# The first weight loads of a two-problem attention kernel: one chunk split over two queues, one moved ahead of a transposing load, two merged

## The chip, the cores and the metric

One core of a Trainium2 chip. The sessions ran on different chips (8, 4 and 1; that of the first result is not on record), and each ratio compares with the kernel before on the same chip. The metric is the device time of one execution in microseconds. In the traces, times count from the start of the span.

## The reference, cut to what matters

Two independent problems, A and B, each grouped-query attention with a key/value cache; only A's first projection, `x @ wq`, matters here. Its contraction over D = 1024 is done in eight chunks of 128.

```python
def _A_ref(x, k_cache, v_cache, wq, wo):      # x: (16, 32, 1024), wq: (1024, 32*128), bf16
    q = (x @ wq).reshape(B, Sq, Hq, Dh).transpose(0, 2, 1, 3)
    k = jnp.repeat(k_cache, rep, axis=1); v = jnp.repeat(v_cache, rep, axis=1)
    p = softmax(einsum("bhqd,bhkd->bhqk", q, k) * Dh ** -0.5)
    o = einsum("bhqk,bhkd->bhqd", p, v)
    return o.transpose(0, 2, 1, 3).reshape(B, Sq, Hq * Dh) @ wo
# ... B the same; the two results side by side
```

## The kernel before: the parts that matter

`w0` holds the weights of the first eight heads (NF = 6, then 6 and 7), `xT` the transposed x. Chunks 0 and 1 of x are transposed by TensorE, the others by transposing loads. ScalarE and SyncE issue loads.

```python
load_x(TT // 2, TT, nc.scalar)
nc.scalar.preload_act_table_set("natural_log_exp_and_others")
load_x(0, TT // 2)
load_w0(0, 1, 0, NF // 2)                 # chunk 0, heads 0-2, SyncE
load_w0(0, 1, NF // 2, NF, nc.scalar)     # chunk 0, heads 3-5, ScalarE
load_w0(1, 2, 0, NF)                      # chunk 1            "w1"
load_w0(2, 3, 0, NF, nc.scalar)           # chunk 2            "w2"
load_x_transposed(2)                      # x, chunks 2 and 3  "xT2"
load_w0(3, 4, 0, NF)                      # chunk 3            "w3"
load_w0(0, HC, NF, REP)                   # heads 6, 7 of chunks 0-3
load_w0(HC, HC + 1, 0, REP)               # chunk 4            "w4"
load_x_transposed(HC)                     # x, chunks 4 and 5  "xT4"
load_w0(HC + 1, DC - 1, 0, REP)           # chunks 5 and 6
load_x_transposed(HC + 2)                 # x, chunks 6 and 7  "xT6"
load_w0(DC - 1, DC, 0, REP)               # chunk 7
...                                       # [cut: later weights, K, V]
warm_up(22)                               # 22 matmuls on a constant
...                                       # [cut: transposes of chunks 0 and 1 of x]
first_heads(range(NF // 2, NF), (0,))     # [cut: heads 0-2 of chunk 0, in two halves]
first_heads(range(NF), (1, 2, 3))         # six matmuls per chunk
first_heads(range(NF, REP), range(HC))    # heads 6, 7: eight matmuls
first_heads(range(REP), range(HC, DC - 1))  # eight per chunk
...                                       # [cut: chunk 7, copies; then heads 8 to 31 among the attention work]
```

## Time and profile before

| | before |
|---|---|
| time, median of the first 3 runs | 343.4 us (343.21 to 343.67) |
| span of the profiled execution | 341.1 us |
| TensorE busy | 334.5 us, 98% |
| first matmul of chunk 1 / of head 8 | 6.28 / 18.80 us |

To read profile lines: PE is TensorE's matmuls, PEld its weight loads, ACT ScalarE, DVE VectorE, POOL GpSimd, SP SyncE; a q marks the engine's queue of instructions, and "issue" in a chain is time in which nothing that the profile shows was waited for. TensorE is the bound from end to end, so a change pays only where TensorE waits. The prediction below shows the only wait on data, 0.6 us for w1. SyncE's queue gives the order of issue (start, us, queue, line, operation; x2 merges two issues):

```profile
0.74 0.45 SPq L465 DMA_DIRECT2D x_sb<-in_A_x_dram  x1
1.26 0.92 SPq L474 DMA_DIRECT2D w_sb<-in_A_wq_dram  x2
2.22 1.44 SPq L468 DMA_TRANSPOSE xT<-in_A_x_dram  x1
3.71 1.60 SPq L474 DMA_DIRECT2D w_sb<-in_A_wq_dram  x3
5.35 1.47 SPq L468 DMA_TRANSPOSE xT<-in_A_x_dram  x1
```

All of these are issued long before their data is used; what decides is when they land.

### The profile page before, as it was taken

To read this page: it belongs to the slowest core of one execution; us is meant where nothing else is said; L and a number is where in the kernel's file an instruction comes from. 1 tells how busy PE (TensorE), PEld (TensorE's weight loads), DVE (VectorE), ACT (ScalarE), POOL (GpSimd) and SP (SyncE) were. 2 spreads that over 40 slices of the span, in tenths; PEclk is the share of its full clock that TensorE was granted. 3 is DMA by queue.
4 is the path that set the end of the run, shared out by engine and by line. 5 is a ranking of instruction groups with operands and counts; after the bars stand their busy time and mean duration, and the time that the engine had idled before them with its cause. 6 is when DMAs were issued, how large, how long until landed. Compare 5 with 4: busy or idle time off the path is not lost.

```text
span 341.1 us, 5436 instructions
## 1 busy us (share of the span) xinstructions
PE 334.5 (98%) x2074; PEld 212.8 (62%) x2113; DVE 265.4 (78%) x335; ACT 185.3 (54%) x208; POOL 47.0 (14%) x206
## 2 busy tenths in 40 slices
PE   8999999999999999999999999999999999999996
PEld 5455666666666666666666666666666666666555
DVE  0047988888988898888888988879888888889540
ACT  2057666666667667666645545555554555555110
POOL 0001110011111111110012221222122101111100
PEclk9999999999999999999999999999999999999999
DMA  7999999999996998899999955998449995430001
GB/s 199 298 188 274 288 250 225 205 254 250 301 258 144 241 222 232 197 294 308 322 293 290 240 125 147 338 284 222 118 106 307 357 194 152 115 93 9 17 19 33
DMA packets 128622, 71.70 MB, mean 210 GB/s; under 512 B 76880, under 2 KB 127824, under 8 KB 128592
## 3 DMA queue, kind: packets, MB, share of 16 engines
q1 hardware_dynamic: 127504, 69.78, 82.5%
q0 software_dynamic: 384, 1.05, 0.8%
q10 hardware_dynamic: 704, 0.49, 0.5%
q8 instruction: 17, 0.28, 0.3%
q14 instruction: 13, 0.11, 0.1%
HBM read 50.59 MB, written 2.10 MB: 154 GB/s over the span
## 4 chain that ended last, share of the span: by engine, by line
PE 96%; DMA 2%; issue 1%; ACT 0%; SPq 0%; ACTq 0%
PE f_ps L320 31%; PE q_ps L301 28%; PE ob L425 17%; PE s_ps L357 16%; PE q_ps L531 4%; DMA w_sb<-in_A_wq_dram 1%; DMA out_dram<-o_sb 0%; ACT o_sb L329 0%; SPq L465 0%; SPq L474 0%; ACTq L329 0%; ACT p_sb L365 0%; ACTq L365 0%
## 5 line engine op out<-in xcount | busy, mean ns | idle before, releaser
L365 ACT ACTIVATE p_sb<-s_ps,shift 128x1024 bf16<-128x1024 f32 x128 | 142.7, 1115 | 97.5 <-PE s_ps L357 86.3
L376 DVE TRANSPOSE_TENSOR_REDUCE parts<-p_sb 128x32 f32<-128x1024 bf16 x128 | 158.7, 1240 | 20.8 <-ACT p_sb L365 19.3
L320 PE MATMUL f_ps<-wo_sb,oT 128*128 128x512 bf16 (+1 forms) x524 | 127.6, 366 | 0.6
L301 PE MATMUL q_ps<-xT,wq_sb 128*128 128x512 bf16 x430 | 113.0, 379 | 0.6
L425 PE MATMUL ob<-p_sb,v_sb 128*128 128x256 bf16 x512 | 76.8, 273 | 0.8
L357 PE MATMUL s_ps<-qT,kT 128*128 128x256 bf16 x512 | 76.8, 273 | 0.0
L320 PEld LDWEIGHTS <-oT 128*128 128x128 bf16 x544 | 53.2, 98 | 35.3
L357 PEld LDWEIGHTS <-kT 128*128 128x128 bf16 x512 | 56.9, 113 | 28.3
L301 PEld LDWEIGHTS <-wq_sb 128*128 128x128 bf16 x448 | 43.8, 98 | 32.2
L425 PEld LDWEIGHTS <-v_sb 128*128 128x128 bf16 x512 | 50.1, 98 | 20.0
L447 DVE TENSOR_TENSOR oT<-r,ob 128x512 bf16<-128x512 f32 x64 | 43.9, 686 | 19.8 <-PE ob L425 19.4
L411 DVE STREAM_TRANSPOSE r<-rall 128x512 f32<-128x512 f32 x64 | 44.2, 691 | 1.1
L309 ACT CAST qT<-q_ps 128x512 bf16<-128x512 f32 x56 | 32.7, 583 | 16.5 <-PE q_ps L301 16.5
L394 POOL COPY half<-cs 64x32 f32<-64x32 f32 x32 | 6.6, 206 | 231.5 <-DVE cs L384 231.4
L329 ACT CAST o_sb<-f_ps 128x512 bf16<-128x512 f32 (+1 forms) x17 | 9.5, 559 | 23.6 <-PE f_ps L320 23.6
L531 PE MATMUL q_ps<-xT,w_sb 128*128 128x512 bf16 (+1 forms) x66 | 14.1, 369 | 0.6 <-DMA w_sb<-in_A_wq_dram 0.6
L406 DVE RECIPROCAL rall<-sums 128x32 f32<-128x32 f32 x32 | 10.4, 326 | 3.3 <-POOL sums L403 3.3
L384 DVE TENSOR_REDUCE cs<-parts 128x32 f32<-128x128 f32 x32 | 12.1, 377 | 1.1
L553 DVE CAST qT<-q_ps 128x512 bf16<-128x512 f32 x4 | 2.5, 683 | 13.2 <-PE q_ps L531 13.2
L531 PEld LDWEIGHTS <-w_sb 128*128 128x128 bf16 x67 | 6.4, 97 | 8.0 <-DMA w_sb<-in_A_wq_dram 1.1
L553 ACT CAST qT<-q_ps 128x512 bf16<-128x512 f32 x4 | 2.1, 599 | 12.8 <-PE q_ps L531 12.8
L331 POOL DMA_DIRECT2D out_dram<-o_sb x8 | 4.6, 575 | 29.2 <-ACT o_sb L329 29.2
(25 smaller groups left out, 48.1 us busy)
## 6 DMA issues: line engine op xcount, KB each, us to landing
v_sb<-in_A_v_cache_dram SPq DMA_DIRECT2D x16, 512.0 KB, 5.4
wq_sb<-in_B_wq_dram SPq DMA_DIRECT2D x8, 1024.0 KB, 6.0
wo_sb<-in_A_wo_dram SPq DMA_DIRECT2D x8, 1024.0 KB, 7.5
v_sb<-in_B_v_cache_dram SPq DMA_DIRECT2D x16, 512.0 KB, 4.6
wo_sb<-in_B_wo_dram SPq DMA_DIRECT2D x8, 1024.0 KB, 8.5
wq_sb<-in_A_wq_dram SPq DMA_DIRECT2D x5, 1024.0 KB, 6.7
wq_sb<-in_A_wq_dram SPq DMA_DIRECT2D x2, 512.0 KB, 7.3
kT<-in_A_k_cache_dram SPq DMA_TRANSPOSE x64, 4.4
```

The costliest lines, as they stand in the source:

```text
L301: nc.tensor.matmul(ps[:], lhsT=w[:, dc, (h % 4) * DH:(h % 4 + 1) * DH], rhs=xT[pr][:, dc, :], start=(dc == 0), stop=(dc == DC - 1),)
L309: nc.scalar.copy(out=qT[pr, g][:, :, hl, :], in_=ps[:].rearrange("p (b s) -> p b s", s=SQ),)
L320: nc.tensor.matmul(ps[:, 0:width], lhsT=oT[pr, tt][:, h, :], rhs=wo_tiles[pr, nh, h // REP][:, h % REP, off:off + width], start=(h == 0), ...
L357: nc.tensor.matmul(s_ps[:, c, :], lhsT=kT[:, i % GRP, c, :], rhs=qT[pr, g][:, b, :, :].rearrange("p h s -> p (h s)"), start=True, stop=True,)
L365: nc.scalar.activation(out=p_sb[:], in_=s_ps[:], func=ACTF.Exp, bias=shift[:], scale=SCALE)
L376: nc.vector.tensor_reduce(out=parts[k][:, q, :, :].rearrange("p c h -> p (c h)"), in_=st[i]["p"][:].rearrange("p c (h s) -> p (c h) s", s=SQ),
L384: nc.vector.tensor_reduce(out=cs[:], in_=parts.pop(k)[:].rearrange("p q c h -> p q h c"), axis=AX.X, op=ALU.add,)
L406: nc.vector.reciprocal(out=rall[:, k, :], in_=quad.pop(k)[:])
L411: nc.vector.transpose(out=r[:].rearrange("p n s -> p (n s)"), in_=rall[:, k, o * 2 * REP:(o + 1) * 2 * REP] .unsqueeze(2).to_broadcast([P, ...
L425: nc.tensor.matmul(ob[j][:, q, :], lhsT=v_sb[:, i % GRP, c, :], rhs=st[i]["p"][:, c, :], start=(c == 0), stop=(c == KC - 1),)
L447: nc.vector.tensor_tensor(out=out, in0=rcp.pop(j)[:].rearrange("p (q h) s -> p q h s", h=REP), in1=ob.pop(j)[:].rearrange("p q (h s) -> p ...
L531: nc.tensor.matmul(first_q[h][:, ts], lhsT=w0[dc // HC][:, dc % HC, h * DH:(h + 1) * DH], rhs=xT[0][:, dc, ts], start=(dc == 0 and t0 == 0 ...
```

## The change

The intent: w1 is what TensorE waits for, and it shares the DMA engines with w2, so bring w1 in with both queues at once and w2 behind it. Chunks 5, 6 and 7 become one load.

```diff
-            load_w0(1, 2, 0, NF)
-            load_w0(2, 3, 0, NF, nc.scalar)
+            load_w0(1, 2, 0, NF // 2)
+            load_w0(1, 2, NF // 2, NF, nc.scalar)
+            load_w0(2, 3, 0, NF)
             load_x_transposed(2)
... [cut: three unchanged loads]
             load_x_transposed(HC)
-            load_w0(HC + 1, DC - 1, 0, REP)
+            load_w0(HC + 1, DC, 0, REP)
             load_x_transposed(HC + 2)
-            load_w0(DC - 1, DC, 0, REP)
```

## The prediction

> **What bounds the kernel now.** I read the page first, then the list of waits, the chain of waits over the first 20 us, and the DMA view in narrow windows. The page:
>
> ```profile
> PE 334.5 (98%) x2074; PEld 212.8 (62%) x2113; DVE 265.4 (78%) x335; ACT 185.3 (54%) x208; POOL 47.0 (14%) x206
> ...
> PE 96%; DMA 2%; issue 1%; ACT 0%; SPq 0%; ACTq 0%
> ```
>
> TensorE is the bound: busy 98% of the 341.1 us span, and 96% of the chain that ended last. The change touches no matmul, only first loads, so it can win only TensorE's idle time. The list of waits of TensorE (waiter, releaser, us in total, times, longest) is two lines long:
>
> ```profile
> PE q_ps L513 <- PEq L687: 0.9, 1, 0.9
> PE q_ps L531 <- DMA w_sb<-in_A_wq_dram: 0.6, 1, 0.6
> ```
>
> The 0.9 us is the start before the warm-up. The 0.6 us is what the change aims at; in the chain (start, us, what) it is:
>
> ```profile
> 1.75 4.48 DMA w_sb<-in_A_wq_dram
> 6.23 0.05 issue
> 6.28 2.33 PE q_ps L531 x10
> 8.61 0.05 issue
> 8.66 10.31 PE q_ps L531 x47
> ```
>
> A load issued at 1.75 us, the second chunk's rows (192 KB on SyncE), lands at 6.23; from 6.28 on TensorE runs without a break. Later delays of loads are hidden now. I name chunks 0 to 7 of the projection's contraction: w1 is the second chunk's weights, w2 the third's, xT2 the transposing load of chunks 2 and 3 of x.
>
> Of the DMA view, windows holding one issue each give KB and us from issue to landing. The lines that carry the argument, in order of issue (the 256 KB one issued at 4.80 and the second transpose at 5.35 share a window):
>
> ```profile
> w_sb<-in_A_wq_dram ACTq DMA_DIRECT2D x1, 96.0 KB, 3.0
> ...
> w_sb<-in_A_wq_dram SPq DMA_DIRECT2D x1, 192.0 KB, 4.5
> w_sb<-in_A_wq_dram ACTq DMA_DIRECT2D x1, 192.0 KB, 4.7
> ...
> xT<-in_A_x_dram SPq DMA_TRANSPOSE x1, 5.2
> ...
> w_sb<-in_A_wq_dram SPq DMA_DIRECT2D x1, 256.0 KB, 5.0
> xT<-in_A_x_dram SPq DMA_TRANSPOSE x1, 5.5
> ...
> w_sb<-in_A_wq_dram SPq DMA_DIRECT2D x1, 512.0 KB, 5.5
> ```
>
> Added to the issue times of the timeline (1.34, 1.75, 1.83, 2.22, 4.80, 5.35, 6.87) they land at: w0's second half 4.34, w1 6.2, w2 6.5, xT2 7.4, w4 9.8, xT4 10.85, w5 with w6 12.4. So w1, issued first, lands only 0.3 us before w2: they moved side by side. What the engines moved per stretch (last two columns: DMA share, GB/s):
>
> ```profile
> 3.00:4.00 1.00, 1.00 (x11) 0.68 (x9) 0.17 (x1) 0.00 (x0) 0.00 (x0) 1.00 0.99 323
> ...
> 5.00:6.00 1.00, 0.68 (x4) 0.10 (x1) 0.00 (x0) 0.00 (x0) 0.00 (x0) 1.00 1.19 195
> ```
>
> The engines are full in both, but from 5 to 6 us, where w2 on ScalarE's queue runs against xT2 on SyncE's, they move 195 GB/s in place of 323.
>
> **What the Trainium skill says.** "DMA: Bandwidth & Descriptors", section "Issuing engines are not separate DMA queues": all issuers use the same 16 DMA engines and interleave, so a second issuer saves only issue time. Section "Queues, rings and completion order": each engine takes turns between rows, packet by packet. The trace agrees: w1 and w2, one per queue, land together. Splitting w1 thus makes no bandwidth; what helps is that w2 no longer takes half of it while w1 is awaited. The same page, "Latency and other measured facts", gives a transposing load 261 GB/s; here xT4 landed 1.05 us behind w4, 262 kB in 1.05 us or 250 GB/s, so it agrees. "Perfetto Trace Analysis", section "Tensor Engine Instruction (MATMUL, LD_WEIGHTS)": a matmul's end is an estimate. It shows: a 512-column matmul is written 379 ns long, but 58 of them started between 6.28 and 18.80, which is 0.216 us each. I count in 0.216.
>
> **The change, part by part.**
>
> (1) What there is to win. The last matmul of chunk 0 starts at 5.29 (end 5.67 less its modelled 0.38). The next could start at 5.29 + 0.216 = 5.51, and started at 6.28. Ceiling: **0.77 us**, a little more than the 0.6 listed.
>
> (2) w1 earlier. Its halves (96 KB each) follow the two halves of w0 in the two queues, with nothing beside them. 197 kB at the 323 GB/s of the row above is 0.6 us after 4.34: lands near 4.95. Chunk 1 starts at 5.51, not held by data: the 0.77 us go.
>
> (3) The next demand is chunk 2, six matmuls later: 5.51 + 6 x 0.216 = 6.81. It needs w2 and xT2. w2 now precedes xT2 in SyncE's queue: another 0.6, near 5.6. xT2 is issued one plain issue (about 0.46 us) later, at 2.7, but its bytes waited for the engines anyway. Undisturbed it takes the 1.05 us of xT4: 5.6 + 1.05 = 6.65. As a check, w1, w2 and xT2 took 7.42 - 4.34 = 3.08 us before; my sum is 2.25 to 2.3, the saving being the slow stretch. I add 0.1 to 0.4 for what I cannot resolve: xT2 at 6.75 to 7.05. Before, chunk 2 started at 6.28 + 1.30 = 7.57; now near 7.0, **a gain of 0.5 to 0.6**, part of the 0.77 being taken by xT2.
>
> (4) Chunk 5 now waits for a merged load, w5 to w7 (768 KB for 512 KB). Its extra 256 KB at the rate of the 512 KB (1.5 us between the landings of xT4 and w5/w6) cost 0.75 us: 12.4 + 0.75 less the 0.4 to 0.6 the stream is ahead, near 12.65. Need: 28 matmuls after chunk 2 starts (6 + 6 + 8 for heads 6 and 7 + 8 of chunk 4), 7.0 + 28 x 0.216 = 13.05. Free, by 0.4 only. Chunk 6's transpose, now behind w7, lands near 13.6, needed at 14.8: free.
>
> (5) SyncE: one issue fewer (about 0.58 us), ScalarE: the same count. Every load keeps its place in time from the next weights on. Bytes and matmuls are unchanged. The tightest later load I found, the 1 MB issued at 20.46, landed at 26.2 and is needed near 27.2, a margin of 1 us. So the gain of the start should reach the end undiminished, as TensorE waits for nothing afterwards.
>
> Sum: 343.4 - 0.5 = **342.9 us**.
>
> **The rivals.**
> (a) xT2 takes the place of w1 as the wait. For it: it is issued 0.46 later, and chunk 2 wants it 0.77 earlier. If it landed at 7.42 as before, 0.15 us would be won (343.25); if the later issue went through in full (7.88), 0.3 would be lost (343.7). Against: the queue, not the issue, held it, since 5.2 us passed from issue to landing and the later transposes do no better.
> (b) The merged w5 to w7 becomes the wait. For it: the thin 0.4 us of (4), and semaphores that need the slowest DMA engine. Against: the stream runs ahead. A late engine there could cost 0.2 to 1 us (343.1 to 343.9).
> (c) The load is hidden anyway, or the gain is lost at a later load. Against: TensorE did wait, and has no second wait to fall into. It would leave 343.4.
> (d) Everything works and xT2 is in time: 0.77 us, 342.6.
>
> **Range and chances.** (d) and the full loss of (a) are about 1.1 us apart and the three times of before spread over 0.46 us, so 342.5 to 343.5 should hold it 8 times in 10. Even the ceiling is 0.2% of the time, a tenth of the threshold: faster by 2% is impossible by this account, slower by 2% needs 7 us and only an unseen fault gives it.
>
> **What would show it.** In the changed profile: the DMA view should have both halves of w1 landing near 5.0; the chain should no longer hold a 4.5 us load of weights, but perhaps a short wait for xT; chunk 1 should start near 5.5 and chunk 2 near 7.0; the projections of head 8 should start near 18.25 rather than 18.80; no wait in the middle of the first projections at 12.5 to 13.5. A wait of TensorE for xT that ends after 7.4, or one for weights near 13, makes the prediction wrong; so does a span that does not follow the start of head 8.

## The result, and the profile after

| | before | after |
|---|---|---|
| median, 6 runs each | 343.31 us (342.94 to 343.67) | 343.27 us (342.7 to 343.92) |
| ratio after / before | | 0.9999, interval 0.9986 to 1.0012 |
| span of the profiled execution | 341.1 us | 341.5 us |
| first matmul of head 8 | 18.80 us | 19.20 us |

The range held (342.5 to 343.5), but the half microsecond forecast at its centre is not there. The page of the changed kernel, TensorE and the chain that ended last:

```profile
PE 335.3 (98%) x2074; PEld 213.3 (62%) x2113; DVE 265.4 (78%) x335; ACT 185.4 (54%) x208; POOL 47.1 (14%) x206
...
PE 95%; DMA 2%; issue 1%; SPq 1%; ACT 0%; ACTq 0%
```

The list of TensorE's waits has lost its second line:

```profile
PE q_ps L513 <- PEq L687: 0.9, 1, 0.9
```

One might call that success. The chain of waits says otherwise (start, us, what):

```profile
2.64 0.04 issue
2.69 5.25 DMA xT<-in_A_x_dram
7.93 0.04 issue
7.98 1.02 PE q_ps L531 x4
```

A DMA is in the chain again: xT2 in place of w1. It lands at 7.93, and chunk 2 starts at 7.98, where the kernel before started it at 7.58. The wait list does not show it because a matmul's modelled end (379 ns for one that takes 216 ns of the array) covers a short wait. The DMA view, windows of one or two issues (KB, us to landing):

```profile
w_sb<-in_A_wq_dram SPq DMA_DIRECT2D x1, 96.0 KB, 4.6
w_sb<-in_A_wq_dram ACTq DMA_DIRECT2D x1, 96.0 KB, 4.7
...
w_sb<-in_A_wq_dram SPq DMA_DIRECT2D x1, 192.0 KB, 4.7
xT<-in_A_x_dram SPq DMA_TRANSPOSE x1, 5.2
```

Half the bytes took as long as the whole before: the halves of w1, issued at 1.75 and 1.83, landed at 6.3 and 6.5, where w1 had landed at 6.2. And the slow stretch that the prediction laid to w2 running against xT2 is still there (TensorE alone, then its clock, DMA share, GB/s):

```profile
4.00:5.00 1.00, 1.00 (x8) 1.00 0.66 170
5.00:6.00 1.00, 1.00 (x5) 1.00 1.78 250
6.00:7.00 1.00, 1.00 (x6) 1.00 0.63 131
```

One more difference sits in TensorE itself. Weight loads of the stretch from 4.2 to 6.4 us (count, busy us, mean ns), the kernel before:

```profile
L531 PEld LDWEIGHTS <-w_sb 128*128 128x128 bf16 x10 | 0.9, 96 | 1.3 <-DMA w_sb<-in_A_wq_dram 1.1
```

and the changed kernel:

```profile
L531 PEld LDWEIGHTS <-w_sb 128*128 128x128 bf16 x10 | 1.3, 141 | 1.1 <-DMA w_sb<-in_A_wq_dram 0.4 <-issue 0.3
```

The same instruction takes 96 ns in one and mostly 151 in the other. TensorE ran chunk 0 slower in this execution, though no instruction of it was changed. One trace of each kernel was evidently not enough.

### The profile page after: what moved, and what is told of

It reads as the page before. It is cut to its first block, busy times and chain, and to the rows that moved or that the text cites. A ratio compares the mean times of both kernels' runs of the same rounds, so it can differ in the third digit from the quotient of the medians.

```text
span 341.5 us, 5437 instructions
## 1 busy us (share of the span) xinstructions
PE 335.3 (98%) x2074; PEld 213.3 (62%) x2113; DVE 265.4 (78%) x335; ACT 185.4 (54%) x208; POOL 47.1 (14%) x206
## 3 DMA queue, kind: packets, MB, share of 16 engines
q0 software_dynamic: 384, 1.05, 0.8%
## 4 chain that ended last, share of the span: by engine, by line
PE 95%; DMA 2%; issue 1%; SPq 1%; ACT 0%; ACTq 0%
PE f_ps L320 31%; PE q_ps L301 28%; PE ob L425 17%; PE s_ps L357 16%; PE q_ps L531 3%; DMA xT<-in_A_x_dram 2%; DMA out_dram<-o_sb 0%; SPq L474 0%; ACT o_sb L329 0%; SPq L465 0%; ACTq L329 0%; ACT p_sb L365 0%; ACTq L365 0%
## 5 line engine op out<-in xcount | busy, mean ns | idle before, releaser
L447 DVE TENSOR_TENSOR oT<-r,ob 128x512 bf16<-128x512 f32 x64 | 43.9, 686 | 19.8 <-PE ob L425 19.4
L531 PE MATMUL q_ps<-xT,w_sb 128*128 128x512 bf16 (+1 forms) x66 | 15.1, 388 | 0.2
```

Of the source, the lines that this page charges most:

```text
L447: nc.vector.tensor_tensor(out=out, in0=rcp.pop(j)[:].rearrange("p (q h) s -> p q h s", h=REP), in1=ob.pop(j)[:].rearrange("p q (h s) -> p ...
L531: nc.tensor.matmul(first_q[h][:, ts], lhsT=w0[dc // HC][:, dc % HC, h * DH:(h + 1) * DH], rhs=xT[0][:, dc, ts], start=(dc == 0 and t0 == 0 ...
```

## The experiments

Twelve more runs were made, all correct: each of the two kernels twice again, and eight variants. Two theories were to be told apart. **Theory one:** xT2 is the new wait because of its own cost: it slows whatever is beside it and is issued later. **Theory two:** the start is slow and uneven by itself; the order of the loads only decides which load the unevenness hits, and TensorE's own start varies too. All traces are summed up in one table; I read the starts from the records of the matmuls, and a load's landing from the last of its 16 completion counts. The second column is the start of the last weight load that took over 140 ns.

| trace | last slow load | w1 landed | xT2 | w3 | w4 | chunk 1 starts | chunk 2 | chunk 3 | chunk 5 | head 8 | span |
|---|---|---|---|---|---|---|---|---|---|---|---|
| before | 3.59 | 6.23 | 7.39 | 8.21 | 9.77 | 6.28 | 7.58 | 8.88 | 13.62 | 18.80 | 341.1 |
| before_again | 6.39 | 6.26 | 7.38 | 8.10 | 9.84 | 6.80 | 8.09 | 9.39 | 14.14 | 19.32 | 341.6 |
| before_third | 5.80 | 6.09 | 7.17 | 8.19 | 9.72 | 6.40 | 7.69 | 8.99 | 13.74 | 18.92 | 341.2 |
| merge_only | 6.45 | 6.19 | 7.34 | 7.85 | 9.70 | 6.74 | 8.04 | 9.33 | 14.08 | 19.26 | 341.6 |
| after | 5.81 | 6.34, 6.53 | 7.93 | 8.57 | 10.27 | 6.39 | 7.98 | 9.27 | 14.02 | 19.20 | 341.5 |
| after_again | 4.38 | 6.32, 6.49 | 7.84 | 8.55 | 10.25 | 6.37 | 7.88 | 9.18 | 15.13 | 20.32 | 342.6 |
| after_third | 4.31 | 4.88, 5.50 | 6.62 | 8.69 | 10.29 | 5.61 | 6.91 | 8.73 | 13.81 | 19.00 | 341.3 |
| after_no_merge | 5.16 | 4.83, 5.62 | 6.75 | 8.88 | 10.51 | 5.98 | 7.27 | 8.93 | 13.69 | 18.87 | 341.6 |
| w2_sync_only | 5.13 | 5.58 | 7.23 | 9.03 | 10.51 | 6.04 | 7.34 | 9.08 | 13.84 | 19.02 | 341.3 |
| split_only | 4.59 | 5.54, 5.80 | 6.66 | 8.85 | 10.31 | 5.73 | 8.66 | 9.97 | 14.72 | 19.90 | 342.6 |
| split_both | 5.16 | 5.01, 5.28 | 7.68 | 8.06 | 9.79 | 6.00 | 7.73 | 9.02 | 13.77 | 18.95 | 341.6 |
| early_transpose | 3.98 | 6.84, 5.41 | 6.57 | 8.40 | 10.10 | 6.89 | 8.19 | 9.49 | 15.71 | 20.90 | 343.2 |
| late_transpose | 6.36 | 5.82, 6.01 | 9.21 | 7.22 | 10.06 | 6.79 | 9.25 | 10.54 | 15.36 | 20.56 | 342.9 |
| all_sync | 3.45 | 5.48 | 7.36 | 8.54 | 10.04 | 6.14 | 7.44 | 8.73 | 13.48 | 18.66 | 341.1 |

**Everything is decided before head 8.** In ten of the fourteen traces the span less the start of head 8 is between 322.3 and 322.4 us; from head 8 to the last matmul all fourteen take 318.96 us. after_no_merge, split_only and split_both end 0.35 to 0.45 us later, after the last matmul (all_sync: 322.44). This goes with the number of transfers that a program issues: these three issue 177 or 178, all others 175 or 176. Why is open, but their ratios below contain it, so they overstate what their start lost. A trace of the start says what the load order did.

**A rival that is not tested: the chip.** before_again, after_again, late_transpose and early_transpose ran on chip 8, merge_only, after_no_merge, w2_sync_only and split_only on chip 4, split_both, all_sync, before_third and after_third on chip 1. With w1 split or w2 out of its way (early_transpose, where xT2 goes first, left aside), w1 landed at 5.8 to 6.5 us in after and on chip 8, and at 4.8 to 5.8 on chips 4 and 1. What sets after_third apart from the other two traces of the changed kernel may thus be the chip and not the run; as far as the record tells, no kernel was traced twice on one chip.

### The two kernels again: before_again, before_third, after_again, after_third

No edit. Expected of the kernel before:

> The kernel before, unchanged, for a second trace of the same start. If the start is the same each time: second chunk's weights (w1) land at 6.2 us, chunk 1 starts at 6.3, chunk 2 at 7.6, the first matmul of head 8 starts at 18.8. If the start varies from run to run by some tenths of a microsecond (the theory that explains why the changed kernel's times spread over 1.2 us): one of these moves by over 0.2 us, and the moment at which a weight load in TensorE's first microseconds drops from 151 to about 96 ns (3.9 us in the first trace of this kernel, 6.2 us in that of the changed one) moves too.

> The kernel before once more, for its spread. From its two traces: w1 lands at 6.2 to 6.3, the fifth chunk's weights (w4) at 9.7 to 9.9, head 8 between 18.8 and 19.3 by the moment TensorE's weight loads speed up (3.6 and 6.4 us so far), and the span is head 8's start plus 322.3.

The start does vary. The chain of before_again has no load in it at all, and neither has that of before_third:

```profile
0.93 2.52 PE q_ps L513 x22
3.45 1.02 PE xT_ps L521 x8
4.47 4.66 PE q_ps L531 x19
```

The warm-up, the transposes, and straight into the projection. Its weight loads of 4.2 to 6.4 us tell why:

```profile
L531 PEld LDWEIGHTS <-w_sb 128*128 128x128 bf16 x10 | 1.5, 151 | 0.9 <-issue 0.3 <-DMA w_sb<-in_A_wq_dram 0.3
```

TensorE went slow until 6.4 us (matmuls of 256 columns started 0.21 us apart, against 0.11 in before) and finished chunk 0 at about 6.8, after w1 had landed (6.26). The Trainium skill, "TensorE: Matmul & The Clock Gate", section "Part 1: The HAM clock gate", gives the mechanism: the array runs at half clock until about 3.4 us of sustained work lie in a free-running window, so the moment depends on the run. The traces agree that it does: the last slow load started between 3.45 and 6.45 us, with the first matmul at 0.93 each time. So **the wait that the change removes was present in one of four traces** with the old order of the first loads (before, before_again, before_third, merge_only). In the other three TensorE itself was late, and no order of the loads from w1 on could have started chunk 1 earlier. The expected span (head 8 plus 322.3) and w4 (9.7 to 9.9) held.

Of the changed kernel:

> The changed kernel, unchanged, for a second trace and a tighter interval. Theory one (the transposing load xT2 is the new wait and lands later because it is issued later): xT2 lands again near 7.9 us, chunk 2 starts near 8.0, head 8 near 19.2, and the mean time is 0.2 to 0.4 us above the kernel before (ratio 1.0006 to 1.0012). Rival (the first trace was one unlucky start, the true gain is the predicted half microsecond): xT2 below 7.3, head 8 below 18.6, ratio 0.998 to 0.999.

> The changed kernel once more, for its spread. From its two traces: xT2 at 7.8 to 7.9, w4 at 10.2 to 10.3 (0.4 to 0.5 later than the kernel before), head 8 at 19.2 or later; the span is head 8's start plus 322.3. If instead w1 lands below 5.7 as in two of the variants: xT2 near 6.8 and a wait for the fourth chunk's weights near 8.9.

after_again, five rounds: 343.57 us median against 343.09, ratio 1.0011 (0.9997 to 1.0025). The predicted ratio, 342.9/343.4 = 0.9985, lies outside. Its list of waits:

```profile
PE q_ps L513 <- PEq L687: 0.9, 1, 0.9
PE q_ps L531 <- DMA xT<-in_A_x_dram: 0.7, 1, 0.7
PE q_ps L531 <- DMA w_sb<-in_A_wq_dram: 0.7, 2, 0.5
```

and the end of its chain:

```profile
7.61 7.47 DMA w_sb<-in_A_wq_dram
15.08 0.05 issue
15.13 5.35 PE q_ps L531 x24
```

The load of 7.61 to 15.08 is the merged one, chunks 5 to 7. Before it, xT4 landed at 13.04 (10.7 to 11.0 in the kernel before) and held chunk 4. In xT4's packet records some 19 packets of 256 bytes that began at 10.1 to 10.3 us all ended at 11.03 to 11.12: 0.74 to 0.92 us each in place of the usual 18 ns. after_third shows the third possibility: w1 at 4.88 and 5.50, xT2 at 6.62, as predicted, chunk 2 at 6.91; then w3 at 8.69 holds chunk 3 until 8.73, and the merged load (13.77) holds chunk 5:

```profile
6.99 6.78 DMA w_sb<-in_A_wq_dram
13.77 0.05 issue
13.81 5.35 PE q_ps L531 x24
```

With no wait, 58 matmuls lie between chunk 1 and head 8: 12.5 us in each trace of the kernel before (18.80 - 6.28, 19.32 - 6.80, 18.92 - 6.40). The changed kernel needed 12.8, 13.95 and 13.4. It started chunk 1 at 6.12 on average against 6.49, 0.37 earlier, and lost 0.3 to 1.4 on the way. Three traces each: a direction, not a mean.

### late_transpose: xT2 out of the slow stretch

```diff
 load_w0(2, 3, 0, NF)
-load_x_transposed(2)
 load_w0(3, 4, 0, NF)
 load_w0(0, HC, NF, REP)
+load_x_transposed(2)
 load_w0(HC, HC + 1, 0, REP)
```

> The changed kernel with the transposing load xT2 moved behind the weights of the fourth chunk and of heads 6 and 7. Theory one (the slow stretch of 4 to 7 us, in which the engines moved 130 to 250 GB/s, is made by the transposing load: some engines take it up early and hold until the last engine has come to it): without it there, w1 lands below 5.4, w2 below 6.1 and the fourth chunk's weights below 6.8 us, and the engines move about 300 GB/s from 4 to 6 us. Rival (the start itself is slow, whatever is loaded): w1 stays at 6.2 to 6.6 and w2 at 6.5 to 7. In both the time rises, as chunk 2 must wait for xT2: it would land near 8.5 to 9, the time up by 0.5 to 1.5 us.

344.62 us against 343.09, ratio 1.0049 (1.0034 to 1.0065): slower, as either theory had it. w1 landed at 5.8 and 6.0, w2 at 6.5, w3 at 7.2: earlier than in after, but well short of theory one's 5.4, 6.1 and 6.8. The rates of 4 to 6 us:

```profile
4.00:5.00 1.00, 1.00 (x9) 1.00 0.98 208
5.00:6.00 1.00, 1.00 (x6) 1.00 0.85 224
```

xT2's packets began at 6.7 us here, and 4 to 6 us is slow all the same. In this trace theory one's main cause falls. What is left is uneven engines. The Trainium skill, "DMA: Bandwidth & Descriptors", section "Why a DMA increments its semaphore by 16 and not by 1", says that a load counts as landed only when all of its engines have counted. The trace shows what that costs: of the 16 engines on w1's SyncE half, fourteen were done by 4.64, two at 5.75 and 5.82. In before, nine were done by 5.04 and seven came at 6.14 to 6.23. Single packets of plain rows, 36 or 65 ns as a rule, took up to 1158 ns in this stretch. Why, no run here shows.

The packet records also show what xT2's landing follows. In eleven of the fourteen traces some packets of xT2 (3 to 19, over 250 ns each) stood and then ended together, 0.18 to 0.24 us after the last plain row before them had ended; xT2 landed 1.2 to 1.3 us after that. In before they began from 5.14 us on and ended at 6.11 to 6.13, with the last row at 5.93; in after from 5.54, 6.72 to 6.76, last row 6.52; in after_third from 5.03, 5.41 to 5.43, last row 5.22. (early_transpose: 0.08 us; all_sync: 0.33; in split_both half of w2 was still running.) So the holding that theory one supposed is there, but behind a late row: by this reading one late engine holds the whole transposing load. It is read from the order in time; the records don't name the engine of a packet, and no run delayed a row on purpose.

### early_transpose: xT2 ahead of w1

```diff
+load_x_transposed(2)
 load_w0(1, 2, 0, NF // 2)
 load_w0(1, 2, NF // 2, NF, nc.scalar)
 load_w0(2, 3, 0, NF)
-load_x_transposed(2)
```

> The changed kernel with the transposing load xT2 issued ahead of the second chunk's weights on SyncE. Theory one (a transposing load needs all engines and holds plain rows behind it): w1's SyncE half lands after xT2, both between 5.6 and 6.6; TensorE waits for w1 as in the kernel before, and w2 lands near 7, just in time or 0.3 late; time within 0.3 us of the kernel before. Rival (the first loads are slow whatever their order): xT2 lands at 6.5 or later and w1 after 7, time up by 0.7 us or more.

xT2 landed at 6.57, w1's SyncE half at 6.84, w2 at 7.50, so TensorE waited for w1. 344.03 us, ratio 1.0019 (1.0005 to 1.0033). By load times it lies between the two expectations, by time nearer the rival. In its profiled execution xT4 came at 13.6 and the merged load at 15.7, as in after_again.

### One part at a time

merge_only: the kernel before with the merged load alone.

```diff
-load_w0(HC + 1, DC - 1, 0, REP)
+load_w0(HC + 1, DC, 0, REP)
 load_x_transposed(HC + 2)
-load_w0(DC - 1, DC, 0, REP)
```

> The kernel before with only the last part of the change: the weights of chunks 5 to 7 in one load of 768 KB ahead of the last transposing load. If the merged load is what ate the gain: TensorE waits for it at chunk 5 (a gap between 12.5 and 14.5 us), head 8 starts 0.3 us or more after the 18.8 to 19.3 of the kernel before, ratio 1.001 or above. If it is free, as the prediction had it: no gap there, ratio within 0.0005 of 1.

Ratio 1.0008 (0.9994 to 1.0021), between the two expectations. The merged load landed at 13.10, against 12.2 to 12.4 for chunks 5 and 6 alone: 0.7 to 0.9 later, close to the predicted 0.75. Needed at 14.08, it held nothing in this trace. It does in the changed kernel, which wants it sooner and gets it later.

after_no_merge: the changed kernel with the last part undone (the diff above, reversed).

> The changed kernel without the last part: chunks 5 and 6 in one load and chunk 7 in another, as before. If the first parts win the predicted half microsecond and the merge gives it back: ratio 0.998 to 0.999. If the transposing load xT2, issued later, takes back what the split gives: xT2 lands at 7.8 to 8.0 as in both traces of the changed kernel, chunk 2 starts near 8, and the ratio is 1.000 to 1.001.

Ratio 1.0015 (1.0001 to 1.0028), or about 0.5 us, of which some 0.4 lie behind the last matmul if that holds in every execution: the start was about as in the kernel before, and no gain was hidden by the merge. xT2 landed at 6.75, which neither expectation had, and then w3 at 8.88 held chunk 3 by about 0.35.

w2_sync_only: w1 whole, w2 on SyncE behind it.

```diff
 load_w0(1, 2, 0, NF)
-load_w0(2, 3, 0, NF, nc.scalar)
+load_w0(2, 3, 0, NF)
 load_x_transposed(2)
```

> The kernel before with only the third chunk's weights (w2) moved to SyncE ahead of xT2, w1 whole. w1 then has the engines to itself after w0. If two queues side by side held w1 back (the prediction's step 2), w1 lands near 5.0 to 5.4. If single late engines in the first 6 us hold it, whatever runs beside it, w1 lands at 5.8 to 6.3 as in all traces so far, and xT2 near 7.8.

Ratio 1.0002 (0.9988 to 1.0015). Fifteen of w1's engines were done by 4.96, the last at 5.58, between the two expectations; xT2 at 7.23. Then w3: fourteen engines by 7.77, the last two at 8.67 and 9.03. The chain:

```profile
4.08 4.96 DMA w_sb<-in_A_wq_dram
9.03 0.05 issue
9.08 10.10 PE q_ps L531 x46
```

Chunk 1 early, chunk 3 late, nothing won.

split_only: w1 split, w2 behind its half on ScalarE.

```diff
-load_w0(1, 2, 0, NF)
+load_w0(1, 2, 0, NF // 2)
+load_w0(1, 2, NF // 2, NF, nc.scalar)
 load_w0(2, 3, 0, NF, nc.scalar)
```

> The kernel before with only w1 split over the two queues, w2 behind it on ScalarE. xT2 is issued early (2.2 us) as in the kernel before. If the later issue of xT2 is what makes it land at 7.9: it lands at 7.3 to 7.5 here, chunk 2 starts by 7.6. If the order of the bytes on the two queues makes it: 7.7 to 8.0 here too. Ratio within 0.001 of 1 either way.

Both expectations missed: xT2 landed at 6.66, and ratio 1.0032 (1.0019 to 1.0046) is a real loss, about 1.1 us, 0.4 of it behind the last matmul. TensorE's waits:

```profile
PE q_ps L532 <- DMA w_sb<-in_A_wq_dram: 1.5, 1, 1.5
```

It waited for w2: fifteen engines were done by 7.16, one at 8.62. But the edit did one thing more: ScalarE issued w2 only at 3.73 us (1.83 in the kernel before), where it waited for the semaphore of its load of x, which landed at 3.72. And all five executions were slow (344.04 to 344.55 us), so one engine that was late in one run does not explain it; how much is due to the late issue is not separated.

### Two candidates: split_both and all_sync

split_both (on the kernel before): w1 and w2 both in halves, ahead of xT2. all_sync: no first load on ScalarE at all.

```diff
 # split_both
-load_w0(1, 2, 0, NF)
-load_w0(2, 3, 0, NF, nc.scalar)
+load_w0(1, 2, 0, NF // 2)
+load_w0(1, 2, NF // 2, NF, nc.scalar)
+load_w0(2, 3, 0, NF // 2)
+load_w0(2, 3, NF // 2, NF, nc.scalar)
 # all_sync
-load_x(TT // 2, TT, nc.scalar)
 load_x(0, TT // 2)
-load_w0(0, 1, 0, NF // 2)
-load_w0(0, 1, NF // 2, NF, nc.scalar)
+load_x(TT // 2, TT)
+load_w0(0, 1, 0, NF)
 load_w0(1, 2, 0, NF)
-load_w0(2, 3, 0, NF, nc.scalar)
+load_w0(2, 3, 0, NF)
```

> A candidate to beat both kernels: w1 and then w2 each in two halves, one per queue, then xT2; the rest as in the kernel before. The two queues carry equal bytes before xT2 as in the kernel before. If the order of bytes is all that counts: w1 near 5, w2 near 5.8, xT2 near 6.8, and head 8 starts below 18.6 in the trace; ratio 0.998 to 0.9995. If single late engines put the lost time back somewhere in the first 9 us whatever the order, and the moment TensorE's clock rises sets the rest: head 8 between 18.8 and 19.9, ratio 1.000 to 1.002.

> The kernel before with every one of the first loads on SyncE, none on ScalarE, w1 and w2 whole and ahead of xT2. If turns between two queues make the long packets and the late engines: w1 and w2 land with all 16 engines within 0.3 us, no plain-row packet before xT2 takes over 250 ns, and the engines move over 300 GB/s from 4 to 6 us. If they come anyway: long packets between 3.7 and 6.2 us as in the other traces, and a spread of over 0.5 us between the engines of w1 or w2.

split_both: ratio 1.0018 (1.0004 to 1.0033), no improvement; w1 early (5.0 and 5.3), xT2 at 7.68 the next wait. Its second half of w2 was held like w2 in split_only: issued at 3.46, with x at 3.44. all_sync shows, in one trace, that taking turns between two queues is not what delays single engines: packets of up to 628 ns before xT2, and w2's engines spread from 5.12 to 6.11. The rates of 4 to 6 us (xT2's first packets began at 4.86 here):

```profile
4.00:5.00 1.00, 0.26 (x4) 1.00 0.96 326
5.00:6.00 1.00, 1.00 (x9) 1.00 1.00 174
```

Its head 8 at 18.66 is the earliest of all, with the clock up at 3.5 us; one look at 342.89 us, inside the range of the kernel before in the same rounds (342.36 to 343.5), so whether it beats both is open.

## Why the prediction was right, and where it was not

**The range was right, and the bound too.** TensorE carries the chain, the ceiling is 0.2% of the time, nothing after head 8 moves, and the gain or loss of the start reaches the end one for one. But the range is 1 us wide and holds the time of no change at all (343.4), so that it held says nothing for the mechanism, and here it was luck: the five times of after_again have their median at 343.57, outside. By the prediction's own sign, "a wait of TensorE for xT that ends after 7.4, or one for weights near 13, makes the prediction wrong", each of the three traces contradicts it in one point or both (xT2 at 7.93 and 7.84; the merged load at 15.08 and 13.77).

**Step 1, the ceiling of 0.77 us, failed as a mean.** It was read off one execution in which TensorE's clock rose early (last slow load at 3.59). In three of four traces with the old first loads it rose at 5.8 to 6.45, chunk 0 ended at 6.4 to 6.8 and w1 was there. The ceiling is 0.77 in one kind of run and about zero in the others. The sum then took the gain from the wrong time: the traced execution, with its wait, took 342.92 us, about what the sum forecast without the wait, because the sum started from the median of 343.4.

**Step 2, "lands near 4.95", failed in two of three traces** of the changed kernel (6.3 to 6.5) and held roughly in one (4.88 and 5.50). Its reason, that w1 was slow because w2 took half of the engines, is not the main one: with nothing beside it but its own other half, w1 could still be late, by a minority of engines. (In part it holds: in w2_sync_only fifteen of w1's engines were done by 4.96, in before nine by 5.04.)

**Step 3, xT2 at 6.75 to 7.05, is the step that should have carried the gain.** In after_third it came at 6.62. In the other two it came at 7.93 and 7.84, which is the number of rival (a): "if the later issue went through in full (7.88), 0.3 would be lost". Its reason is not shown: after_third issued xT2 at the same 2.69. In all three traces xT2 landed 0.9 to 1.0 us after w2 (6.94, 6.86, 5.74), about the 1.05 that the prediction allowed; the term that failed is w2's landing, "near 5.6". Chunk 2 then started 0.3 to 0.4 later than in the trace it was reckoned from. The reasoning that the slow stretch of 4 to 7 us was made by w2 against xT2, so that its 0.8 us could be saved, failed too: late_transpose is slow from 4 to 6 us with no such pair.

**Step 4 and rival (b).** The cost of the merge was right (0.7 to 0.9 against 0.75), and the note that the margin was thin was right. "Free" was wrong in two of three traces: chunk 5 waited for it in after_again and after_third. The load stream was not 0.4 to 0.6 ahead as assumed but behind: w4 landed at 10.25 to 10.29 in all three traces of the changed kernel, at 9.70 to 9.84 in the four with the old first loads. Why the new order makes it half a microsecond later is not settled. Fewer bytes on ScalarE's queue would fit w2_sync_only (10.51) and split_both (9.79, as many bytes there as before), but not split_only (10.31, with more). A later issue (4.69 to 4.90 us with the old first loads, 5.16 to 5.37 in the changed kernel) fits no better: split_both 5.16, split_only 4.81.

**Step 5**, that nothing later takes the gain back, was right of the time from head 8 on. Its count of issues was wrong: SyncE issues as many loads as before (164 in each; w2 came, chunk 7's went), not one fewer.

**Sum.** What came earlier at chunk 1 was 0.37 us on average over three traces, and 0.3 to 1.4 us went to xT2, w3, xT4 or the merged load, a different one each time. Taking 322.3 us from the recorded spans gives an estimate of head 8 for every execution: 18.6 to 20.3 for the twelve of the changed kernel, 18.3 to 19.4 for the 29 of the kernel before that have a span; the forecast was 18.25. All twelve times of the changed kernel average 343.44 us (standard deviation 0.50), all 35 of the kernel before in these sessions 343.18 (0.27). That comparison is not by common rounds, so it is only a hint of a small loss; the wider spread fits a start that hangs more often on a late engine.

## What to carry to other kernels

Before you compute the gain from a wait, take a second and a third trace of the same kernel: a wait of half a microsecond at the start may belong to the run and not to the program. Take the gain from the time of the traced execution, and trace both kernels on one chip. When loads fill the DMA engines, moving one forward can move later ones back (w4 here, 9.7 to 9.8 against 10.25 to 10.29), so list the landing and the demand of the next five loads and not of one. A short wait can hide from a list of waits under a matmul's modelled end; the chain and the start times of consecutive matmuls show it.

## What the Trainium skill lacked or had wrong

- "TensorE: Matmul & The Clock Gate", section "Part 1: The HAM clock gate": it says that the transition point varies by ±500 ns and calls the count run-variable. Here the last slow weight load started anywhere from 3.45 to 6.45 us over fourteen traces, a spread of 3.0 us, with the first matmul always at 0.93. In all_sync it started only 2.5 us after the first matmul, less than the page's 3.4 us.
- "DMA: Bandwidth & Descriptors" does not say that single plain-row packets of 36 or 65 ns can take up to 1.6 us (w2_sync_only, at 6.57 us) with nothing but this kernel's loads, nor that one or two engines of 16 then end a load 1.2 to 1.5 us after the rest (w2 in split_only, 7.16 against 8.62). Its nearest rows, in "Latency and other measured facts", are an HBM latency of 2 us at high load and engines 7 and 15 as usually slower; the records here don't name the engine, so neither could be tested.
- The same page, "DMA Transpose (X-bar)": it does not say that the packets of one transposing load can stop together and be released together (19 packets of xT4 in after_again, 0.74 to 0.92 us each, all ended within 0.1 us; 3 to 19 of xT2 in eleven traces, 0.18 to 0.24 us after the last plain row). The page's 261 GB/s, in "Latency and other measured facts" for a non-contiguous middle dimension, fits an undisturbed one (250 here), but xT4 in that run landed 2.8 us after w4, where 1.05 was undisturbed.
- "Perfetto Trace Analysis", section "Tensor Engine Instruction (MATMUL, LD_WEIGHTS)": right that ends are modelled; it could add that a list of idle times made from them misses waits. Chunk 2 of after waited for xT2 by some 0.3 us (started 7.98; six matmuls after 6.39 it could have started at 7.69) and the list showed none.
